# One run of small products per unit instead of two, and a reordered last group, in a linear-attention + maxout-FFN kernel

## The chip, the cores and the metric

The kernel runs on one core of a Trainium2 chip. The metric is the device time of one execution in microseconds (us); the page and the times speak of the same program, and the profiled execution has its own time. Engines are named as in the profile: PE is TensorE (matmuls), PEld its weight loads, DVE is VectorE, ACT is ScalarE, POOL is GpSimd, SP is SyncE, which here issues most of the DMAs. A label such as L870 is a line of the kernel before.

## The reference

A gated linear recurrence over 4 batches x 8 heads x 768 tokens with head size 48, followed by a feed-forward layer with a maximum of three products over the 3072 tokens that come out:

```python
f = 1 / (1 + exp(-f_logit))
for t in range(S):
    state = f[:, :, t, :, None] * state + einsum('bhd,bhe->bhde', k[:, :, t], v[:, :, t])
    y[:, :, t] = einsum('bhd,bhde->bhe', q[:, :, t], state)
x = y.transpose(0, 2, 1, 3).reshape(B * S, H * D)          # 3072 x 384
h = max(x @ w1, x @ w2, x @ w3)                            # 384 -> 768
out = h @ w_out                                            # 768 -> 384
```

## The kernel before, in words

**Units.** The recurrence is cut into chunks of 64 tokens. A unit `u` is one chunk of two batches with all eight heads; there are 24 units (`NU`), and four units make a group (`GRP`) of 512 tokens, the block that the feed-forward layer works on. Within a unit, the products of gates give scaled keys `kh` and queries `qh` (scans on DVE, multiplications on POOL from unit 6 on). With them PE does four kinds of small product, 16 matmuls each, all in fp32 with 48 or 64 rows and 64 columns, so that four of them lie in the array at a time:

- `pairs(u)` (L392): k times q inside the chunk, into the PSUM tile `a`; DVE multiplies it with the causal mask and writes `at` (L395).
- `values(u)` (L411): `at` times v, which begins the output tile `y`.
- `sums(u)` (L436): the sum over the chunk of k times v. DVE adds it to the decayed state and writes the new state (L444); `carry` (L357, POOL) makes the decayed state for the unit after the next.
- `finish(u)` (L500): the old state times `qh`, added to `y` in PSUM, and then three ACT copies (L506) of `y` into the group's input `xT`.

After a group's last unit, `pack` moves a part of `xT` by DMA (L519), and the group is ready for the feed-forward layer.

**The feed-forward work** is a generator, `ffn`. Its first half `inputs_by_pairs` (matmuls at L870) computes the three products and their maximum in a Strassen-like form with three output blocks `n`: DVE reads banks at L913 (`third`), L920 and L921 (`fourth`), ACT reads them at L878 to L905, and POOL makes sums of the result `hm` (L603). Its second half `outputs_by_pairs` (matmuls at L631, ACT reads at L636, DVE reads at L639) multiplies by `w_out`. It begins with products that need only the blocks 0 and 1 of `hm`; the "rest" products that need block 2 follow, then the sums `s1` into the banks `c` and (in the last group) `b`, then `s2` into the bank `a`, a read of `a` (`read(a, 1)`), and further products into `a`.

**Order.** Every engine works through its own queue in the order in which this program writes it. `fill(ns)` takes steps out of the pending `ffn` until a budget is used up; one fill is about 2.4 us of PE work, and a group's `ffn` is spread over 20 of them, five to a unit. In the loop over units before the change, one unit is: fill; blocks of transposed keys (L382, DVE); `finish(u-1)` and `pairs(u)`; loads; the scan for the next unit; fill; `kh` and `qh` for the next unit; fill; `values(u)` and `sums(u)`; `carry`; two more fills. So PE meets two runs of small products per unit, `finish`+`pairs` and `values`+`sums`, with two to three fills of large products between them. In the last two units there are no sums, and there `values` is followed by an ACT copy of one element, `seen` (L420), which the later `finish` has to wait for because it writes the same place of `y`. After the loop come a fill, `finish(23)`, a `pack` on two queues, and then the last group's `ffn`, between whose steps range checks of the weights (ACT, L278 and L280) are put.

[...] The loads are issued by SP in one long queue.

Of the kernel before, what the change touches and what calls it, by code (L numbers as in the profile page):

```python
# [9 lines left out]
FP32 = mybir.dt.float32  # L10
# [36 lines left out]
C = 64  # L47
# [8 lines left out]
def kernel(  # L56
# [13 lines left out]
    B, H, S, D = q.shape  # L70
    HP = H // 2
    NU = B // 2 * (S // C)
    UT = 2 * C
# [4 lines left out]
    GRP = 4  # L78
# [11 lines left out]
    def fast():  # L90
        ctx = ExitStack()
        with ctx:
# [65 lines left out]
            both = (nc.sync, nc.scalar)  # L158
# [213 lines left out]
            def keys_by_blocks(u, n):  # L372

                if BY_ROWS <= u < NU - 2:
                    kh = ready[u]["kh"]
                    if n == 0:
                        ready[u]["ks"] = work.tile([UT, H, DP], FP32, name="ks")
                    ks = ready[u]["ks"].rearrange("s (hp par) d -> s hp par d", par=2)
                    a, t0 = divmod(n * 32, C)
                    for p0 in range(0, 128, 32):  # L380
                        par, e0 = divmod(p0, DP)
                        nc.vector.transpose(ks[n * 32:(n + 1) * 32, :, par, e0:e0 + 32], kh[p0:p0 + 32, :, a, t0:t0 + 32])  # L382

            FOUR = [(par, a) for a in range(2) for par in range(2)]

            def pairs(u):
                kh, qh = ready[u]["kh"], ready[u]["qh"]
                p = ps_a.tile([UT, 2, 512], FP32, name="a")
                for hp in range(HP):
                    for par, a in FOUR:  # L390
                        r, t = slice(par * DP, par * DP + D), slice(a * C, (a + 1) * C)
                        nc.tensor.matmul(p[t, par, hp * C:(hp + 1) * C], lhsT=kh[r, hp, a, :], rhs=qh[r, a, hp, :],  # L392
                                         start=True, stop=True)
                at = work.tile([UT, 2, HP, C], FP32, name="at")
                nc.vector.tensor_tensor(at, p[:, :, 0:HP * C].rearrange("s par (h t) -> s par h t", h=HP),  # L395
                                        mask.unsqueeze(1).unsqueeze(1).to_broadcast([UT, 2, HP, C]), op=ALU.mult)
                ready[u]["at"] = at

            def values(u):
                d = ready[u]  # L400
                v_ld = v_tiles[u % NLD]
                y = ps_y.tile([128, 2, 512], FP32, name="y")
                for hp in range(HP):
                    for par, a in FOUR:
                        o, s = (par ^ a) * DP, slice(a * C, (a + 1) * C)
                        if u < GRP:
                            nc.tensor.matmul(y[s, par, hp * D:(hp + 1) * D], lhsT=d["at"][s, par, hp, :],
                                             rhs=v_ld[s, 2 * hp + par, 0:D], start=(hp == 0),
                                             stop=False, skip_group_check=True)
                            continue  # L410
                        nc.tensor.matmul(y[o:o + DP, a, hp * C:(hp + 1) * C], lhsT=v_ld[s, 2 * hp + par, :],  # L411
                                         rhs=d["at"][s, par, hp, :], start=(hp == 0),
                                         stop=False, skip_group_check=True)
                d["y"] = y
                if u >= GRP:
                    sums(u)
                if u >= NU - 2:

                    seen = work.tile([1, 1], FP32, name="seen")
                    nc.scalar.copy(seen, y[0:1, 1, (HP - 1) * C:(HP - 1) * C + 1])  # L420

            def sums(u):

                d, v_ld = ready[u], v_tiles[u % NLD]
                y = d["y"]
                if u < NU - 2:


                    apart = u < GRP
                    if apart:  # L430
                        y = ps_a.tile([128, 2, 512], FP32, name="a")
                    Y = HP * C
                    for hp in range(HP):
                        for par, a in FOUR:
                            s = slice(a * C, (a + 1) * C)
                            nc.tensor.matmul(y[par * DP:(par + 1) * DP, a, Y + hp * D:Y + (hp + 1) * D],  # L436
                                             lhsT=d["ks"][s, 2 * hp + par, :], rhs=v_ld[s, 2 * hp + par, 0:D],
                                             start=apart and hp == 0, stop=(hp == HP - 1), skip_group_check=True)
                    ds = y[:, :, Y:Y + HP * D]
                    new = states[u % 2].rearrange("p (a h) d -> p a (h d)", a=2)  # L440
                    if u < 2:
                        nc.scalar.copy(new, ds)
                    else:
                        nc.vector.tensor_tensor(new, ds, d["state"].rearrange("p (a h) d -> p a (h d)", a=2), op=ALU.add)  # L444
# [47 lines left out]
            def finish(u, xT):  # L492
                d = ready[u]
                y = d["y"]
                if u >= 2:
                    st = d["state"].rearrange("p (a h) d -> p a h d", a=2)
                    for hp in range(HP):
                        for par, a in FOUR:
                            r, o = slice(par * DP, par * DP + D), (par ^ a) * DP
                            nc.tensor.matmul(y[o:o + D, a, hp * C:(hp + 1) * C], lhsT=st[r, a, hp, :],  # L500
                                             rhs=d["qh"][r, a, hp, :], start=False, stop=(hp == HP - 1),
                                             skip_group_check=True)
                t0 = u % GRP * UT
                for par, a, n in ((0, 0, 2), (1, 1, 1), (0, 1, 1)):
                    i, o = slice(par * DP, (par + n) * DP), slice((par ^ a) * DP, ((par ^ a) + n) * DP)
                    nc.scalar.copy(xT[o, :, t0 + a * C:t0 + (a + 1) * C],  # L506
                                   y[i, a, 0:HP * C].rearrange("p (h t) -> p h t", h=HP))
                ready.pop(u)
# [105 lines left out]
            def outputs_by_pairs(g, hm, xT):  # L614
# [14 lines left out]
                def into(b, p, lhs, rhs, part=slice(None)):  # L629
                    for x, w in list(zip(lhs(p), rhs))[part]:  # L630
                        nc.tensor.matmul(b[:, p * HD:(p + 1) * HD], lhsT=x, rhs=w, start=id(b) not in begun, stop=True,  # L631
                                         skip_group_check=True)
                        begun.add(id(b))

                def read(b, n):
                    nc.scalar.copy(partial[n], b[:, 0:DM])  # L636

                def add(out, b, n, at=slice(0, 2)):
                    nc.vector.tensor_tensor(out[:, at], pairs_of(b[:, 0:DM])[:, at], pairs_of(partial[n])[:, at], op=ALU.add)  # L639

                PART_COST = HD * COLUMN
                COST, PLAIN = len(order) * PART_COST, len(lin[0]) * PART_COST
                a, b, c = bank(), bank(True), bank(True)
# [21 lines left out]
                    store_part(g, 0, 0)  # L665
                yield 2 * PART_COST
                d = b if last else c
                into(c, 0, s1, T(0))
                yield COST
                if last:  # L670
# [5 lines left out]
                else:  # L676
                    nc.scalar.copy(tops[:, 2], c[:, 0:DM])
                yield COST
                into(a, 0, s2, T(1))
                yield COST  # L680
                into(a, 1, s2, T(1))
                read(a, 1)
                yield COST
                into(a, 0, A(0, 1), T(2))
                yield COST
                into(a, 1, A(0, 1), T(2))
# [294 lines left out]
            with tc.manual_schedule():  # L981
# [78 lines left out]
                for u in range(GRP, NU):  # L1060
# [4 lines left out]
                    fill(part)  # L1065
                    keys(u)
                    keys_by_blocks(u, 2)
                    if u > GRP:
                        finish(u - 1, xT)
                        if u % GRP == 3:  # L1070
                            pack(0, 2, xT)
                        elif u % GRP == 0:
                            pack(3, 3, xT)
                    if u % GRP == 0:
# [1 line left out]
                            packed[u // GRP - 1] = xT  # L1076
                            pending.append(ffn(u // GRP - 1, xT))
                        xT = x_tiles[u // GRP % 2]
                    pairs(u)

                    if u + 2 <= BY_ROWS:
                        load(u + 2)
# [15 lines left out]
                    fill(part)  # L1098
                    if BY_ROWS < u + 2 < NU and u % GRP == 0:
                        load(u + 2, one, "k")  # L1100
                    values(u)
                    if n < NU:
                        carry(n)
                    check_range(u - CHECKS, 1)
                    fill(part)
                    if BY_ROWS < u + 2 < NU and u % GRP == 0:
                        load(u + 2, one, "q")
                    keys_by_blocks(n, 0)
                    fill(part - 1000 if u < 2 * GRP else part)
                    keys_by_blocks(n, 1)  # L1110
# [3 lines left out]
                    if BY_ROWS <= u + 2 < NU:  # L1114
                        sigmoids(u + 2)
                fill(PART)
                finish(NU - 1, xT)
                pack(3, 3, xT, both)
                packed[NU // GRP - 1] = xT
                pending.append(ffn(NU // GRP - 1, xT))  # L1120
                for n in range(NU - CHECKS, len(pieces)):
                    for step in range(3):
# [265 lines left out]
```

## Time and profile before

| what | value |
|---|---|
| median of 4 runs | 416.1 us (415.0 to 417.43) |
| the profiled execution: its own time | 415.51 us |
| its span, first to last instruction | 413.8 us |
| granted TensorE clock | 0.993 |
| PE busy | 398.5 us (96%) |
| PE weight loads busy | 332.8 us (80%) |
| DVE busy | 289.4 us (70%) |
| POOL busy | 243.6 us (59%) |
| ACT busy | 178.2 us (43%) |
| small products, busy: L392, L411, L500, L436 | 15.8, 13.9, 13.3, 11.7 us |

A line of the timeline gives the start, the time from the first start to the last end, the engine, the line, the operation, output<-inputs, shapes and the number of records; one fp32 matmul of PE leaves two records. What stands in brackets is idle time just before the line and what ended it. Matmul ends are modelled, so a cost on PE is read from start to start, and PE can be held up without a bracket.

### The profile page before, as it was taken

What the parts mean: (1) busy time and instruction counts of PE and PEld (TensorE: products, weight loads), DVE (VectorE), ACT (ScalarE), POOL (GpSimd) and SP (SyncE); (2) the same over time, 40 slices, a digit from 0 to 9 for tenths busy, and PEclk for the clock granted to TensorE, in tenths of its full rate; (3) what the DMA queues carried; (4) which work ended last, traced back from release to release, by engine and by line L of the source; (5) the groups of instructions that cost most, each with busy time, mean ns of one, the idle gap of its engine ahead of it and who ended that gap; (6) DMA issues with size and microseconds to landing.
All of it is one profiled execution on the core that took longest, in us unless ns stands there. A gap on an engine that the chain in (4) does not pass through costs nothing.

```text
span 413.8 us, 11546 instructions
## 1 busy us (share of the span) xinstructions
PE 398.5 (96%) x4598; PEld 332.8 (80%) x4598; DVE 289.4 (70%) x569; ACT 178.2 (43%) x412; POOL 243.6 (59%) x270
## 2 busy tenths in 40 slices
PE   4989999999999999999999999999999999999995
PEld 3767775566668889988889988889988898988984
DVE  6986897996775999897888977988894450002500
ACT  2487786511223431444441354523245324576210
POOL 2188694731968887487486376667466850525700
PEclk9999999999999999999999999999999999999998
DMA  8999986777456777277635376724573011641002
GB/s 170 240 274 295 260 205 87 88 150 157 79 114 85 118 129 143 41 115 90 144 78 96 55 115 86 172 56 79 73 153 88 2 55 41 153 135 59 0 21 62
DMA packets 181563, 47.21 MB, mean 114 GB/s; under 512 B 160449, under 2 KB 179201, under 8 KB 181505
## 3 DMA queue, kind: packets, MB, share of 16 engines
q1 hardware_dynamic: 178032, 45.62, 54.6%
q10 hardware_dynamic: 3472, 0.81, 0.9%
q8 instruction: 37, 0.61, 0.6%
q14 instruction: 22, 0.17, 0.2%
HBM read 37.75 MB, written 4.72 MB: 103 GB/s over the span
## 4 chain that ended last, share of the span: by engine, by line
PE 78%; SPq 7%; DVE 5%; DMA 3%; ACT 3%; issue 2%; POOL 1%; ACTq 0%; DVEq 0%; POOLq 0%
PE p L870 16%; PE p L631 14%; PE tr L870 13%; PE tr L631 11%; PE p L537 6%; PE p L563 6%; PE y L411 3%; PE y L500 2%; SPq L183 2%; PE p L776 2%; SPq L174 2%; SPq L164 2%; PE a L392 2%; PE y L436 2%; DVE ks L382 2%
## 5 line engine op out<-in xcount | busy, mean ns | idle before, releaser
L382 DVE STREAM_TRANSPOSE ks<-kh 32x128 f32<-32x128 f32 x256 | 77.4, 302 | 9.2 <-POOL kh L340 5.1
L870 PE MATMUL tr<-xT,placed 128*128 128x256 f32 x300 | 72.7, 385 | 0.2 <-DVE hm L913 0.2
L870 PEld LDWEIGHTS tr<-xT,placed 128*128 128x128 f32 x300 | 55.6, 190 | 9.3 <-ACT hm L878 1.4
L870 PE MATMUL p<-xT,placed 128*128 128x256 f32 x180 | 45.0, 381 | 0.0
L339 POOL COPY ends<-r 128x8 f32<-128x8 f32 x24 | 8.8, 366 | 49.7 <-DVE r L329 49.7
L870 PEld LDWEIGHTS p<-xT,placed 128*128 128x128 f32 x180 | 33.8, 190 | 4.7
L537 PE MATMUL p<-xT,w_in 128*128 128x256 f32 (+1 forms) x108 | 35.1, 470 | 1.5 <-POOL w_in L745 0.7
L329 DVE TENSOR_TENSOR_SCAN r<-gate,from_one 128x520 f32<-128x520 f32 x24 | 32.0, 1333 | 6.0 <-ACT gate L308 2.8
L340 POOL TENSOR_TENSOR kh<-kt,r 128x512 f32<-128x512 f32 x18 | 30.8, 1711 | 8.3 <-DVE kt L296 6.9
L639 DVE TENSOR_TENSOR o<-tr,w_in 128x384 f32<-128x384 f32 (+1 forms) x11 | 5.7, 521 | 38.6 <-PE tr L631 35.1
L603 POOL TENSOR_TENSOR w_in<-hm 128x256 f32<-128x256 f32 x15 | 11.1, 738 | 34.9 <-DVE hm L921 32.3
L347 DVE TENSOR_TENSOR_SCAN prod<-gate,from_inv 128x520 f32<-128x520 f32 x24 | 31.1, 1297 | 0.0
L506 ACT COPY xT<-y 64x256 f32<-64x256 f32 (+1 forms) x60 | 22.1, 368 | 19.3 <-PE y L500 18.1
L870 PE MATMUL p<-w_in,placed 128*128 128x256 f32 x120 | 30.0, 379 | 0.0
L913 DVE TENSOR_TENSOR hm<-tr,hm 128x512 f32<-128x512 f32 x15 | 10.3, 688 | 26.6 <-PE tr L870 19.7
L537 PEld LDWEIGHTS p<-xT,w_in 128*128 128x128 f32 x108 | 20.1, 195 | 10.4 <-issue 6.2
L636 ACT COPY w_in<-p 128x384 f32<-128x384 f32 x15 | 7.2, 477 | 45.8 <-PE p L631 45.8
L631 PE MATMUL p<-w_in,hm 128*128 128x192 f32 x120 | 25.4, 335 | 1.1 <-ACT w_in L636 1.1
L258 POOL TENSOR_TENSOR w_in<-top_bits,rest_bits 128x384 uint32<-128x384 uint32 x18 | 21.6, 1208 | 7.8 <-DVE top_bits L252 3.8
L280 ACT ACTIVATE raw<-top_bits 128x384 f32<-128x384 f32 x48 | 25.2, 526 | 0.4
L870 PEld LDWEIGHTS p<-w_in,placed 128*128 128x128 f32 x120 | 22.8, 190 | 3.1
L631 PE MATMUL tr<-w_out,w_in 128*128 128x192 f32 x120 | 24.4, 326 | 0.0
(159 smaller groups left out, 904.4 us busy)
## 6 DMA issues: line engine op xcount, KB each, us to landing
raw<-in_moe_w_dram SPq DMA_DIRECT2D x24, 384.0 KB, 4.3
v_ld<-in_v_dram SPq DMA_DIRECT2D x48, 96.0 KB, 3.2
placed<-in_moe_w_dram SPq DMA_DIRECT2D x12, 384.0 KB, 5.5
out_dram<-o SPq DMA_DIRECT2D x46, 96.0 KB, 2.2
placed<-in_moe_w_out_dram SPq DMA_DIRECT2D x6, 384.0 KB, 4.7
f_ld<-in_f_logit_dram SPq DMA_DIRECT2D x36, 64.0 KB, 2.9
k_ld<-in_k_dram SPq DMA_DIRECT2D x36, 64.0 KB, 2.8
q_ld<-in_q_dram SPq DMA_DIRECT2D x36, 64.0 KB, 2.7
```

The costliest lines, as they stand in the source:

```text
L258: nc.gpsimd.tensor_tensor(dst, by(top), by(rest), op=ALU.add)
L280: nc.scalar.activation(over, size, AF.Relu, scale=(-1 / HI_MIN, 1.0)[step - 1], bias=(1.0, -HI_END * (1 - 2.0 ** -24))[step - 1], accum_ou ...
L329: nc.vector.tensor_tensor_scan(r[:, 0:LEN][:, ::-1], flat(gate)[:, ::-1], flat(from_one)[:, ::-1], 1.0, op0=ALU.mult, op1=ALU.max)
L340: (nc.vector if u < BY_ROWS else nc.gpsimd).tensor_tensor(kh.rearrange("p h a t -> p a h t"), kt, by_batch(r[:, 1:LEN + 1].rearrange("p (x ...
L347: nc.vector.tensor_tensor_scan(flat(prod), flat(gate_tiles[u % 2]), flat(from_inv[u % 2]), 1.0, op0=ALU.mult, op1=ALU.max)
L382: nc.vector.transpose(ks[n * 32:(n + 1) * 32, :, par, e0:e0 + 32], kh[p0:p0 + 32, :, a, t0:t0 + 32])
L411: nc.tensor.matmul(y[o:o + DP, a, hp * C:(hp + 1) * C], lhsT=v_ld[s, 2 * hp + par, :], rhs=d["at"][s, par, hp, :], start=(hp == 0), stop=F ...
L506: nc.scalar.copy(xT[o, :, t0 + a * C:t0 + (a + 1) * C], y[i, a, 0:HP * C].rearrange("p (h t) -> p h t", h=HP))
L537: nc.tensor.matmul(p if w < TOK else p.rearrange("p (two t) -> p two t", two=2), lhsT=w_in[i][:, kt, j * 128:(j + 1) * 128], rhs=x[:, t.st ...
L563: nc.tensor.matmul(p[:, 0:DM], lhsT=lhsT, rhs=rhs, start=(n == 0), stop=(n == NJ + NK - 1))
L631: nc.tensor.matmul(b[:, p * HD:(p + 1) * HD], lhsT=x, rhs=w, start=id(b) not in begun, stop=True, skip_group_check=True)
L870: nc.tensor.matmul(b[:, j * HALF:(j + 1) * HALF], lhsT=w[:, (2 * n + j) * 128:(2 * n + j + 1) * 128], rhs=x, start=begin and j == 0, stop= ...
```

## The change

It does three things.

1. `values(u-1)` and `sums(u-1)` leave the middle of unit `u-1` and go to the top of unit `u`, into one run: `values(u-1)`, `sums(u-1)`, `pairs(u)`, `finish(u-1)`. For this, the sums go into the free columns of the PSUM tile of `pairs` (`room_of_unit`) instead of those of `y`, and the DVE addition that writes the state is split off (`new_state`) and called inside `finish`, behind the mask multiplication. Since `values` and `finish` now stand in one run, `seen` is issued for every unit from 4 on.
2. In the last unit `values(23)` stays where it was, and `finish(23)` with its `pack` moves two fills ahead, so that two fills and the check steps lie between it and the last `ffn`.
3. In the last group's `outputs_by_pairs`, the two steps of `s2` with `read(a, 1)` (new function `second`) go ahead of the two steps of `s1`. In the other groups the order stays.

```diff
-            def pairs(u):
+            def pairs(u, p=None):
...
-                if u >= GRP:
-                    sums(u)
-                if u >= NU - 2:
+                if u >= GRP:
                     seen = work.tile([1, 1], FP32, name="seen")
                     nc.scalar.copy(seen, y[0:1, 1, (HP - 1) * C:(HP - 1) * C + 1])
...
-            def sums(u):
+            def sums(u, p=None):
...
+                    d["sums"] = y = room_of_pairs() if p is None else p
...
-                                             start=apart and hp == 0, stop=(hp == HP - 1), skip_group_check=True)
+                                             start=True, stop=True)
+                    if p is None:
+                        new_state(u)
...
             def finish(u, xT):
...
+                new_state(u)
...
+                def second():
+                    for p in range(2):
+                        into(a, p, s2, T(1))
+                        if p:
+                            read(a, 1)
+                        yield COST
...
+                if last:
+                    yield from second()
                 into(c, 0, s1, T(0))
...
-                into(a, 0, s2, T(1))
-                yield COST
-                into(a, 1, s2, T(1))
-                read(a, 1)
-                yield COST
+                if not last:
+                    yield from second()
...
                     keys_by_blocks(u, 2)
+                    room_of_unit = room_of_pairs()
+                    if u > GRP:
+                        values(u - 1)
+                        sums(u - 1, room_of_unit)
+                    pairs(u, room_of_unit)
                     if u > GRP:
                         finish(u - 1, xT)
...
-                    pairs(u)
...
-                    values(u)
                     if n < NU:
                         carry(n)
+                    else:
+                        values(u)
...
+                    if n == NU:
+                        finish(u, xT)
+                        pack(3, 3, xT, both)
+                        packed[u // GRP] = xT
...
                 fill(PART)
-                finish(NU - 1, xT)
-                pack(3, 3, xT, both)
-                packed[NU // GRP - 1] = xT
                 pending.append(ffn(NU // GRP - 1, xT))
```

More of the change, by code (lines that the diff above doesn't have):

```diff
@@ L384, in fast, with room_of_pairs @@
             FOUR = [(par, a) for a in range(2) for par in range(2)]
-            def pairs(u):
+            def room_of_pairs():
+                return ps_a.tile([128, 2, 512], FP32, name="a")
+            def pairs(u, p=None):
                 kh, qh = ready[u]["kh"], ready[u]["qh"]
-                p = ps_a.tile([UT, 2, 512], FP32, name="a")
+                if p is None:
+                    p = room_of_pairs()
                 for hp in range(HP):
@@ L415, in values @@
                 if u >= GRP:
-                    sums(u)
-                if u >= NU - 2:
                     seen = work.tile([1, 1], FP32, name="seen")
                     nc.scalar.copy(seen, y[0:1, 1, (HP - 1) * C:(HP - 1) * C + 1])
-            def sums(u):
+            def sums(u, p=None):
                 d, v_ld = ready[u], v_tiles[u % NLD]
-                y = d["y"]
                 if u < NU - 2:
-                    apart = u < GRP
-                    if apart:
-                        y = ps_a.tile([128, 2, 512], FP32, name="a")
+                    d["sums"] = y = room_of_pairs() if p is None else p
                     Y = HP * C
@@ L437, in sums, with new_state @@
                                              lhsT=d["ks"][s, 2 * hp + par, :], rhs=v_ld[s, 2 * hp + par, 0:D],
-                                             start=apart and hp == 0, stop=(hp == HP - 1), skip_group_check=True)
-                    ds = y[:, :, Y:Y + HP * D]
+                                             start=True, stop=True)
+                    if p is None:
+                        new_state(u)
+            def new_state(u):
+                d = ready[u]
+                if u < NU - 2:
+                    ds = d["sums"][:, :, HP * C:HP * (C + D)]
                     new = states[u % 2].rearrange("p (a h) d -> p a (h d)", a=2)
```

## The prediction

> **What bounds the kernel now.** I read the page first: PE is busy 96% of the span, and its waits add up to 9.6 us, 8.3 of them before 50 us. So time is gained only where PE has less to do, or where PE is held up without a bracket.
>
> Second, the timeline of PE over unit 18 and at the two units where `values` stands alone:
>
> ```profile
> 256.06 1.03 PE L870 MATMUL p<-w_in,placed 128*128 128x256 f32 x4
> 257.02 0.66 PE L500 MATMUL y<-qh,state 48*48 48x64 f32 x32
> 257.50 0.65 PE L392 MATMUL a<-qh,kh 48*64 48x64 f32 x32
> 258.08 1.99 PE L870 MATMUL tr<-xT,placed 128*128 128x256 f32 x8
> ...
> 262.50 1.03 PE L870 MATMUL tr<-xT,placed 128*128 128x256 f32 x4
> 263.46 0.69 PE L411 MATMUL y<-at,v_ld 64*64 64x64 f32 x32
> 263.97 0.63 PE L436 MATMUL y<-v_ld,ks 64*64 64x48 f32 x32
> 264.54 1.99 PE L870 MATMUL tr<-xT,placed 128*128 128x256 f32 x8
> 266.37 1.03 PE L870 MATMUL p<-xT,placed 128*128 128x256 f32 x4
> ...
> 336.82 0.49 PE L631 MATMUL tr<-w_in,xT 128*128 128x192 f32 x2
> 337.24 0.69 PE L411 MATMUL y<-at,v_ld 64*64 64x64 f32 x32
> 337.87 0.92 PE L631 MATMUL p<-w_out,hm 128*128 128x192 f32 x4
> 338.62 0.49 PE L631 MATMUL p<-w_in,xT 128*128 128x192 f32 x2
> ```
>
> A large record costs 0.216 us (256 columns) or 0.1625 (192) from start to start. What a run takes beyond the large work beside it: `values`+`sums` from 262.50+4x0.216=263.36 to 266.37-8x0.216=264.64: 1.28 us. `finish`+`pairs`, reckoned likewise: 1.26. `values` alone, 337.145 to 338.62-0.65=337.97: 0.83; the lone `finish(23)` at 346.51: 0.83. So an added `sums` costs 0.45, an added `pairs` 0.43, and a run by itself about 0.33 beyond its products (0.83 against the 0.48 to 0.52 that `finish` or `values` takes to the next product inside a run).
>
> Third, the timelines around 161 us and the end:
>
> ```profile
> 134.68 0.71 DVE L296 STREAM_TRANSPOSE qt<-q_ld 128x512 f32<-128x512 f32 x1 [2.52 <-DMA out_dram<-o]
> ...
> 161.26 0.68 DVE L921 SCALAR_TENSOR_TENSOR hm<-hm,top_bits 128x512 f32<-128x512 f32 x1
> ```
> ```profile
> 160.91 0.49 PE L631 MATMUL tr<-w_in,xT 128*128 128x192 f32 x2
> 161.40 1.20 PE L631 MATMUL p<-w_out,hm 128*128 128x192 f32 x4
> 162.43 0.81 PE L631 MATMUL tr<-w_out,hm 128*128 128x192 f32 x4
> ```
> ```profile
> 398.07 0.48 ACT L636 COPY w_in<-p 128x384 f32<-128x384 f32 x1 [2.28 <-PE p L631]
> 398.60 0.92 PE L631 MATMUL p<-w_in,hm 128*128 128x192 f32 x4 [0.57 <-ACT w_in L636]
> ```
>
> DVE waits 2.52 us for a q load and from 134.68 to 161.94 has no idle line; SP issues loads without a gap from 50 to 140 us, one each 0.6 us, so that load's time does not depend on PE. At 161.40 PE's four "rest" records take 1.03 us instead of 0.65: they wait for `hm` from L920/L921. Here, in unit 11, load queue and DVE hold PE, and what PE saves before it is lost. The last fence: `s2` ends, ACT reads `a`, PE stands 0.57 us.
>
> **The change part by part.**
>
> *The merged run.* One run of four products: 1.28+1.26-0.33=2.21 us. The 0.33 is known at both ends only: 0 if the switching goes on between the products of one run, 0.40 if an inner `values` costs what an inner `pairs` does (0.83-0.43). I take 0.33, read from the same two products.
>
> Before the point at 162 us, DVE's stretch keeps its contents: the state additions L444 of units 9 and 10 (0.52 us each) move inside it, at 135.31 and 148.25, and stay inside it. So the rest products still wait until 161.94, and everything saved in units 5 to 11 goes. So does the new stall of unit 5: there `seen` queues behind five ACT instructions ending with the key copy L369 (68.30 to 68.88); `finish(4)` could start 1.40 us after `values`, at about 68.0, and would start at 69.0. It costs 1.0 us, and the stretch covers it; uncovered, it is added.
>
> From 162 us on, the small work before is: `finish`+`pairs` of unit 12 with its stall, 168.28 to 169.70: 1.42; `values`+`sums` of unit 12, likewise 1.35; nine units of 1.26+1.28=22.86; unit 22, 1.26+0.83; unit 23, 1.26. Together 28.98. After: units 12 to 22, 11x2.21=24.31, and unit 23 without sums, 1.76: 26.07. The lone `values(23)` and `finish(23)` cost the same on both sides. Gain 2.91 us; the part is small because `values(11)` and `sums(11)` now fall behind the point. With 0 saved per merge the same sum is a loss of 1.05, with 0.40 a gain of 3.75.
>
> *The added wait.* `finish(u-1)` waits for `seen`, and `seen` stands in ACT's queue ahead of the copies L506 and all later reads of banks. At 323.06 `values` starts and `seen` runs 323.82 to 323.97, 0.91 after; `finish` follows `values` by 0.52+0.45+0.43=1.40. Slack 0.49, so I cost it at nothing. Before units 16 and 20 ACT also has a 0.48 us read (228.32 to 228.80, from 0.11 into the run); it ends before `values` does. Its cover gone, it costs the excess in each run.
>
> *The moved state addition* now stands ahead of the next unit's scans: 0.52 us later for `qh`. `qh` was ready 1.2 us before `pairs` in units 16 and 20 (227.49 against 228.70) and 2.8 to 6.7 elsewhere after unit 12; `pairs` itself comes 0.48 later in its run, units are 0.33 shorter: 0.8 us left. DVE's `hm` for the rest products of unit 15 had 1.4 us to spare (220.53 against 221.95); the state addition and a PE path shorter by 0.33 leave 0.6. Nothing is charged. At unit 12 `pairs` stands 0.97 into the run and meets `qh` (168.93) without the old stall. SP: `pack` waits for copies that end some 0.9 us later in the run, and loads and stores queue behind it; unit 18's k load was waited for 0.17 us by a DVE chain with 5 us left. POOL's `carry` gets its state half a unit ahead.
>
> *The last unit.* `finish(23)` stood, at 346.51, between `s2` and the product that needs `a` read, and hid that read. Moved, it uncovers the stall that the last group shows: +0.67 (0.57, and 0.10 because the next records start slower after an empty array: 398.60 to 399.35 is 0.75, not 0.65). Against it, the stall of 0.55 at 351.87, where ACT was late behind the L506 copies and a DMA issue of 0.72, shrinks to about 0.1: -0.56.
>
> *The last group.* With `s1` (2.6 us) behind `s2`, the read of `a` is covered: -0.67. But `s2` now follows `read(a, 0)` (392.22 to 392.70), and PE could start it at 392.67: +0.18. The DVE sums of `xT` and POOL's `s2` (389.8) are ready. Both last parts together: +0.11-0.49=-0.38.
>
> Sum: -2.91-0.38=-3.3, on the profiled 415.51 us (span 413.8 and 1.7 around it): 412.2. That execution stands 0.6 below the median, so 412.8.
>
> [...]
>
> L921 of one shape took 684 to 1707 ns in this trace, so the point may move by 1.0 either way.
>
> **The rivals.**
>
> 1. *The point gives way.* For: DVE's stretch contains one 1.71 us L921. Against: the q load's time is SP's. If nothing binds there, 19 merges of 0.33 count, less unit 5's 1.0, plus the last parts: -6.3+1.0-0.4=-5.7, 410.4 us by the median.
> 2. *The switching stays, inside the run* (64-row products next to 48-row ones). For: no row shows these two kinds side by side. +1.05-0.38=+0.7: 416.8 us, no measurable change.
> 3. *Slower: `finish` waits for ACT in each merged run.* Twelve runs after the point each pay what ACT is late beyond 0.49 us; from 0.28 us late the gain is gone. For: ACT does steps of 0.5 to 0.6 us, in order, and unit 5 shows the case. Against: at units 13 to 23 ACT is idle or in its last step at the run's start. At 0.5: +6.0-3.3=+2.7, 418.8 us.
>
> **How the numbers follow.** Forecast 0.55, rival 1 0.12, rival 2 0.18, rival 3 0.15. The forecast's own range is 411.5 to 414.2 (0.25 to 0.40 saved, the point moving by 0.7). Over 0.5% (2.1 us, about what a measurement can tell) is faster below 414.0: most of the forecast (0.50) and rival 1: 0.61; within: the rest of it and rival 2: 0.23; slower: rival 3: 0.16. The range from 410.6 to 417.0 leaves out rival 3 and part of rival 1.
>
> **What would show it.** Right: one run per unit, about 2.2 us by the same reckoning, large products uninterrupted for five fills; L920/L921 of unit 11 and the rest products still near 162 us; no bracket on L500 but in unit 5 and, where ACT waits for L921, unit 11; no wait after the last `s2`, one in group 4. Wrong: brackets or gaps ahead of L500 in every unit, a run of 2.5 us, or rest products well before 161 us.

## The result and the profile after

The changed kernel takes 415.87 us (median of 52 runs, 413.02 to 417.66), the kernel before 416.57 us (78 runs, 414.4 to 419.17). The ratio is 0.9979, interval 0.997 to 0.9988: 0.9 us faster by the ratio, 0.7 by the two medians, and less than the 0.5% from which the prediction would have called it faster. 412.8 us was forecast. The profiled execution took 415.81 us, with a span of 414.1 us against 413.8 before: 0.3 us longer, where the sum of the prediction was 3.3 us shorter.

The merged run itself came out as predicted. The timeline of PE over unit 17 of the kernel after (the columns are those of the lines before: start, time, engine, line, operation, shapes and records, idle time):

```profile
241.93 1.03 PE L881 MATMUL tr<-xT,placed 128*128 128x256 f32 x4
242.89 0.69 PE L415 MATMUL y<-at,v_ld 64*64 64x64 f32 x32
243.40 0.63 PE L433 MATMUL a<-v_ld,ks 64*64 64x48 f32 x32
243.85 0.66 PE L396 MATMUL a<-qh,kh 48*64 48x64 f32 x32
244.34 0.63 PE L504 MATMUL y<-qh,state 48*48 48x64 f32 x32
244.89 1.13 PE L881 MATMUL tr<-xT,placed 128*128 128x256 f32 x4
245.86 1.03 PE L881 MATMUL p<-xT,placed 128*128 128x256 f32 x4
247.26 2.86 PE L881 MATMUL tr<-xT,placed 128*128 128x256 f32 x12 [0.37 <-ACT hm L889]
```

From 241.93+4x0.216=242.79 to 245.86-4x0.216=245.00 is 2.20 us for four products in one run (2.21 predicted), where the two runs before cost 1.26 and 1.28. But the last line shows something that was not there before: eight records behind the run, PE stands 0.37 us for L889, an ACT read of a bank.

The view of PE's waits after, by line and by the line waited for (us in total, times, longest):

```profile
PE y L504 <- ACT seen L422: 2.3, 2, 1.6
...
PE tr L881 <- ACT hm L889: 1.1, 3, 0.4
PE a L396 <- POOL qh L351: 1.0, 1, 1.0
...
PE p L542 <- ACT hm L807: 0.7, 2, 0.3
PE p L636 <- ACT w_in L641: 0.6, 1, 0.6
```

`finish` waits for `seen` twice, in units 5 and 11, not in every unit. In unit 10 `pairs` waits for `qh`, which POOL makes from the q load that DVE waits for. The wait in the last group is gone, one in group 4 is left.

Where the time came from and went is read from the start of the first large record behind the run that has `pairs(u)`, kernel after minus kernel before. The last column compares the two kernels with the obstacles out of the way; it belongs to the experiments.

| at unit | after - before, us | e8_all - e5_late_before, us |
|---|---|---|
| 9 | +0.02 | -0.03 |
| 10 | +0.81 | -0.24 |
| 11 | +2.21 | -0.57 |
| 12 | +2.49 | -0.80 |
| 13 | +2.28 | -0.94 |
| 14 | +2.41 | -1.25 |
| 16 | +1.76 | -1.91 |
| 17 | +1.61 | -2.05 |
| 18 | +1.74 | -2.37 |
| 20 | +1.07 | -3.03 |
| 21 | +0.93 | -3.17 |
| 22 | +1.06 | -3.48 |
| 23 | +0.75 | -3.80 |
| last matmul | +0.32 | -5.09 |

By unit 11 the kernel after is 2.21 us behind; at the point at 162 us 1.71 of that is left, as shown below. At unit 12 it is 2.49, because the run there also holds `values(11)` and `sums(11)`, which the kernel before had done at 158.10, ahead of the point. From unit 12 on it gains 0.33 us per unit, but not in every unit: from 12 to 13, 16 to 17 and 20 to 21 it gains only 0.14 to 0.21, and from 13 to 14, 17 to 18 and 21 to 22 it loses 0.13.

The lines of the kernel after that answer to those around 161 us, first DVE, then PE:

```profile
135.47 0.71 DVE L296 STREAM_TRANSPOSE qt<-q_ld 128x512 f32<-128x512 f32 x1 [3.00 <-DMA out_dram<-o]
...
139.94 1.30 DVE L932 SCALAR_TENSOR_TENSOR hm<-hm,top_bits 128x512 f32<-128x512 f32 x1
...
152.38 1.74 DVE L932 SCALAR_TENSOR_TENSOR hm<-hm,top_bits 128x512 f32<-128x512 f32 x1 [0.35 <-POOL top_bits L917]
...
162.58 0.69 DVE L932 SCALAR_TENSOR_TENSOR hm<-hm,top_bits 128x512 f32<-128x512 f32 x1
```
```profile
154.89 0.97 PE L504 MATMUL y<-qh,state 48*48 48x64 f32 x32 [1.56 <-ACT seen L422]
155.79 2.07 PE L881 MATMUL p<-rest_bits,placed 128*128 128x256 f32 x4
157.65 1.45 PE L881 MATMUL p<-w_in,placed 128*128 128x256 f32 x4
...
163.49 0.81 PE L636 MATMUL p<-w_out,hm 128*128 128x192 f32 x4
164.14 0.81 PE L636 MATMUL tr<-w_out,hm 128*128 128x192 f32 x4
```

The record that stood at 162.43 before now stands at 164.14: 1.71 us later. Three things make it up. The q load is in at 135.47 instead of 134.68, 0.79 later. DVE's stretch from there to the end of the last L932 takes 163.27-135.47=27.80 us instead of 161.94-134.68=27.26, 0.54 more. And PE did not have to wait at 163.49: it came 0.38 us later than DVE would have let it go (the record after L932 followed 0.49 after its end before, 162.43-161.94; 163.27+0.49=163.76 against 164.14). Why PE was late there is told in the last section: its granted clock was 0.50 from 155.4 to 158.4.

### The profile page after: what moved, and what is told of

Read it like the earlier page. It is cut to its first block, busy times and chain, and to the rows that moved or that the text cites. A ratio compares the mean times of both kernels' runs of the same rounds, so it can differ in the third digit from the quotient of the medians.

```text
span 414.1 us, 11516 instructions
## 1 busy us (share of the span) xinstructions
PE 393.1 (95%) x4598; PEld 332.4 (80%) x4598; DVE 295.0 (71%) x569; ACT 180.6 (44%) x430; POOL 246.8 (60%) x270
## 4 chain that ended last, share of the span: by engine, by line
PE 85%; DVE 5%; ACT 3%; POOL 3%; issue 2%; DMA 0%; SPq 0%; DVEq 0%; POOLq 0%; ACTq 0%
PE p L881 17%; PE p L636 15%; PE tr L881 14%; PE tr L636 11%; PE p L542 7%; PE p L568 6%; PE p L787 3%; PE y L415 3%; PE a L396 2%; PE y L504 2%; PE a L433 2%; DVE ks L382 1%; POOL w_in L258 1%; DVE r L329 1%; PE y L411 1%
## 5 line engine op out<-in xcount | busy, mean ns | idle before, releaser
L881 PE MATMUL tr<-xT,placed 128*128 128x256 f32 x300 | 71.6, 384 | 1.1 <-ACT hm L889 1.1
L542 PE MATMUL p<-xT,w_in 128*128 128x256 f32 (+1 forms) x108 | 34.0, 459 | 3.4 <-POOL w_in L756 1.9
L329 DVE TENSOR_TENSOR_SCAN r<-gate,from_one 128x520 f32<-128x520 f32 x24 | 33.0, 1375 | 6.0 <-ACT gate L308 2.8
L542 PEld LDWEIGHTS p<-xT,w_in 128*128 128x128 f32 x108 | 19.5, 190 | 12.7 <-issue 6.0
L641 ACT COPY w_in<-p 128x384 f32<-128x384 f32 x15 | 7.2, 479 | 42.2 <-PE p L636 42.2
```

Source lines behind the costliest of these rows:

```text
L329: nc.vector.tensor_tensor_scan(r[:, 0:LEN][:, ::-1], flat(gate)[:, ::-1], flat(from_one)[:, ::-1], 1.0, op0=ALU.mult, op1=ALU.max)
L542: nc.tensor.matmul(p if w < TOK else p.rearrange("p (two t) -> p two t", two=2), lhsT=w_in[i][:, kt, j * 128:(j + 1) * 128], rhs=x[:, t.st ...
L881: nc.tensor.matmul(b[:, j * HALF:(j + 1) * HALF], lhsT=w[:, (2 * n + j) * 128:(2 * n + j + 1) * 128], rhs=x, start=begin and j == 0, stop= ...
```

## Experiments

All were timed in five rounds beside the kernel before.

**The two parts alone.** e1_merge_only is the kernel after with the old order in the last group:

```diff
-                if last:
-                    yield from second()
                 into(c, 0, s1, T(0))
...
-                if not last:
-                    yield from second()
+                yield from second()
```

e2_tail_only is the kernel before with the new order in the last group:

```diff
+                if last:
+                    into(a, 0, s2, T(1))
+                    yield COST
+                    into(a, 1, s2, T(1))
+                    read(a, 1)
+                    yield COST
                 into(c, 0, s1, T(0))
...
-                into(a, 0, s2, T(1))
...
-                yield COST
...
+                if not last:
+                    into(a, 0, s2, T(1))
+                    yield COST
...
```

> The change without its third part: in the last group s1 stays ahead of s2. Theory (each of the two parts is worth what the rows said): the stall of 0.57 us ahead of the product that follows the last s2 is back and the time is 0.5 us above the changed kernel, some 0.4 us below the kernel before (ratio 0.999). Rival (the reorder is hidden by the end of the kernel, or the merge alone carries the gain): equal to the changed kernel, ratio 0.998.

> The kernel before with the third part alone: s2 ahead of s1 in the last group. Theory: the 0.57 us wait after the last s2 goes, a wait of up to 0.2 us ahead of s2 comes, 0.5 us below the kernel before (ratio 0.9988). Rival: the wait reappears further on in the same group (another read of the same bank, the last store), no difference (1.000).

e1_merge_only: 415.91 us, ratio 0.9986 (0.9969 to 1.0002). e2_tail_only: 416.14 us, ratio 0.9991 (0.9972 to 1.001). Neither time tells from no change; the traces do. The timeline of PE in e1_merge_only has the old wait:

```profile
397.93 0.49 PE L636 MATMUL p<-w_in,w_in 128*128 128x192 f32 x2
398.99 0.92 PE L636 MATMUL p<-w_in,hm 128*128 128x192 f32 x4 [0.57 <-ACT w_in L641]
```

and the kernel after, whose lines have `s1` there, has not:

```profile
398.69 0.49 PE L636 MATMUL tr<-w_out,w_in 128*128 128x192 f32 x2
399.02 0.81 PE L636 MATMUL p<-w_in,hm 128*128 128x192 f32 x4
```

From `finish(23)` to the last matmul it is 67.81 us in e1_merge_only (340.89 to 408.70) and 67.22 in the kernel after (341.41 to 408.63): the last group is worth 0.59, in e2_tail_only against before 61.23 to 61.80: 0.57. Predicted: 0.49.

These two gave something else. In e2_tail_only, which has the order of before at 162 us, the q load came in at 136.61, 1.93 us later than in the profiled execution of before, and its span is 415.1 us:

```profile
136.61 0.71 DVE L296 STREAM_TRANSPOSE qt<-q_ld 128x512 f32<-128x512 f32 x1 [1.78 <-DMA out_dram<-o]
```
```profile
164.36 0.81 PE L631 MATMUL tr<-w_out,hm 128*128 128x192 f32 x4
```

So the load's time is not one number. What the kernels differ in is the way from the load to the record behind the point:

| profiled execution | q load in | record behind the point | between |
|---|---|---|---|
| before | 134.68 | 162.43 | 27.75 |
| e2_tail_only (runs apart) | 136.61 | 164.36 | 27.75 |
| e1_merge_only (merged) | 135.33 | 163.63 | 28.30 |
| e6_check (merged) | 135.59 | 163.86 | 28.27 |
| after (merged) | 135.47 | 164.14 | 28.67 |

The 0.54 of DVE belongs to the merge: it is there in all three merged executions, and not in the two with the runs apart. Nothing ties the 0.79 of the load to the merge: the latest load of the five is in an execution with the runs apart; what sets it stays open. The 0.38 is in one execution alone: in e1_merge_only and e6_check `finish` waited for `seen` just as long (1.55 and 1.53 us), and yet PE was early enough to wait for DVE, as the timeline of PE in e1_merge_only shows:

```profile
154.76 0.67 PE L504 MATMUL y<-qh,state 48*48 48x64 f32 x32 [1.55 <-ACT seen L422]
...
162.60 1.19 PE L636 MATMUL p<-w_out,hm 128*128 128x192 f32 x4 [0.70 <-DVE hm L928]
163.63 0.81 PE L636 MATMUL tr<-w_out,hm 128*128 128x192 f32 x4
```

So the wait for `seen` in unit 11 is covered by DVE's, and costs nothing by itself here.

**The load out of the way.** In both kernels (e4_late_after from the kernel after, e5_late_before from the kernel before) the eight stores of group 0's outputs are put behind later DMAs in SP's queue, so that the k and q loads are issued earlier:

```diff
                             nc.scalar.copy(o, p[:, 0:DM])
-                            store(i, o)
+                            late.append((i, o))
```

> The changed kernel with the first group's eight output stores put off until its q load for units 10 and 11 is issued; nothing else moves, and the q load is issued some 4.6 us earlier. Theory (the SP queue holds DVE until 135 us, DVE holds an ACT read of a bank in unit 11, and seen and finish(10) stand behind that read): the waits of 1.0 us (unit 10) and 1.6 us (unit 11) go and with them 3 to 4.6 us, ratio to the kernel before about 0.989. Rival (the stall at unit 11 is made by the moved state addition and by the run itself, whatever the loads do): the 1.6 us wait stays and less than 1 us is gained, ratio 0.996.

> The kernel before with the same eight stores put off. Theory: it had held-up products of 0.2, 0.2, 0.15, 0.4 and 0.15 us between 137 and 169 us, so it gains about 1.1 us (ratio 0.997), much less than the changed kernel does by the same edit; the difference between the two kernels grows from 0.9 to 3.5 us or more. Rival: the load was no bound in either kernel, both gain the same, 0 to 0.5 us.

e4_late_after: 411.59 us (411.02 to 412.24), ratio 0.9875 (0.9853 to 0.9896), span 410.0. e5_late_before: 414.44 us (413.93 to 414.72), ratio 0.9944 (0.9925 to 0.9962), span 412.7. SP's issue of the q load in the kernel after (the last column counts the DMAs):

```profile
128.69 4.51 SPq L183 DMA_DIRECT2D q_ld<-in_q_dram  x8
```

and in e4_late_after, with DVE's transposition of q and PE's run in unit 11:

```profile
123.78 5.21 SPq L183 DMA_DIRECT2D q_ld<-in_q_dram  x8
```
```profile
131.74 0.71 DVE L296 STREAM_TRANSPOSE qt<-q_ld 128x512 f32<-128x512 f32 x1 [1.63 <-DMA q_ld<-in_q_dram]
```
```profile
150.59 0.69 PE L415 MATMUL y<-at,v_ld 64*64 64x64 f32 x32
...
152.04 0.63 PE L504 MATMUL y<-qh,state 48*48 48x64 f32 x32
152.60 1.13 PE L881 MATMUL p<-rest_bits,placed 128*128 128x256 f32 x4
```

The load is 3.7 us earlier, the waits of units 10 and 11 are gone, and with the load earlier in both kernels the change as a whole, last group included, is worth 414.44-411.59=2.85 us, three times what it brought with it, but less than the 3.5 expected. The kernel before gains 2.2 us by the medians and 1.1 by the spans of the profiled executions (412.7 against 413.8), as expected; the rest may be that the profiled execution of before had an early load.

The load may also be what spreads the times: 12 runs of e2_tail_only lie 4.1 us apart and 52 of the kernel after 4.6 us, but 5 and 6 of these two 1.2 and 0.8 us, and 12 of e13_split below, which has late stores too, 1.2. It is not shown: 12 runs of e1_merge_only, with the load where it was, lie only 2.4 apart, and 5 of e8_all below, with late stores, 1.8.

**The range checks behind a fill.** The waits for L889 follow only the runs of units 13, 17 and 21. The kernel after, ACT in unit 17:

```profile
243.65 0.15 ACT L422 COPY seen<-y 1x1 f32<-1x1 f32 x1 [0.93 <-PE y L415]
245.03 1.13 ACT L511 COPY xT<-y 128x256 f32<-128x256 f32 x3 [1.23 <-PE y L504]
246.18 0.55 ACT L278 ACTIVATE top_bits<-raw 128x384 f32<-128x384 f32 x1
246.64 0.57 ACT L889 COPY hm<-tr 128x512 f32<-128x512 f32 x1
```

and the kernel before:

```profile
242.95 1.13 ACT L506 COPY xT<-y 128x256 f32<-128x256 f32 x3 [0.90 <-PE y L500]
244.10 0.56 ACT L278 ACTIVATE top_bits<-raw 128x384 f32<-128x384 f32 x1
244.57 0.56 ACT L878 COPY hm<-tr 128x512 f32<-128x512 f32 x1
```

Before, `finish` opened the run and `pairs` ran beside the copies, so the read of the bank ended at 245.13, and PE went on at 245.19. Now `finish` closes a run that is nearly twice as long: the copies start 2.14 us after the run did (245.03 against 242.89; before, 242.95 against 242.22, 0.73), the check step stands between them and the read, and PE goes on when the read has ended, at 247.21. e6_check is the kernel after with the check step moved behind the fill:

```diff
+                    fill(part)
                     check_range(u - CHECKS, 0)
-                    fill(part)
```

> The changed kernel with the first step of the range check (an ACT instruction of 0.55 us, L278) written behind the next fill instead of ahead of it. Theory (in units 13, 17 and 21 finish's three ACT copies now end 0.5 us later against PE, the check step stands behind them, and the read of a bank that PE needs for the fifth product stands behind both): the three waits of 0.38 us on that read go, with 0.08 to 0.1 each for the slower restart, 1.4 us in all, ratio to the kernel before 0.9945. Rival (the copies alone make ACT late, the check step is not needed for it): the waits only shrink, under 0.5 us is gained, ratio 0.997.

414.14 us (413.1 to 414.67), ratio 0.9934 (0.9913 to 0.9955), span 412.5. The timeline of PE in unit 17:

```profile
245.13 1.03 PE L881 MATMUL p<-xT,placed 128*128 128x256 f32 x4
246.10 2.86 PE L881 MATMUL tr<-xT,placed 128*128 128x256 f32 x12
```

All three waits are gone. Of the 1.6 us of span, 0.28 was gained at the point (163.86 against 164.14, where the kernel after had been late by its clock) and the rest behind it, 0.43 to 0.44 per wait: 0.37 or 0.38 and a slower restart. So the rival of the expectation, that the copies alone make ACT late, is out.

**The price of a run, by itself.** e13_split is e4_late_after with the merged run cut again, between `sums` and `pairs`, half of the fill on each side:

```diff
-                    fill(part)
+                    fill(part / 2 if u > GRP else part)
                     keys(u)
...
                         sums(u - 1, room_of_unit)
+                        fill(part / 2)
                     pairs(u, room_of_unit)
```

> The changed kernel with the late stores, and the merged run cut in two: half of the unit's first fill stands between the sums and the pairs, so that PE does the same work in the same queue order but for large products between the two halves of each of 19 runs. Theory (a run costs 0.33 us beyond its products, paid where PE changes between small and large products): 19 x 0.33 = 6.3 us more than with the late stores alone (411.6), some 417.5 us, ratio 1.002. Rival (the gain of the late stores comes from other waits, and a run by itself costs next to nothing): within 1 us of 411.6 us, ratio 0.988 to 0.99.

416.96 us (416.84 to 418.04), ratio 1.0012 (0.9997 to 1.0028), span 415.2: 5.2 us more than e4_late_after by the spans, 5.4 by the medians. The timeline of PE in unit 16:

```profile
225.65 0.49 PE L636 MATMUL p<-w_in,w_in 128*128 128x192 f32 x2
226.07 0.70 PE L415 MATMUL y<-at,v_ld 64*64 64x64 f32 x32
226.59 0.63 PE L433 MATMUL a<-v_ld,ks 64*64 64x48 f32 x32
227.15 0.92 PE L636 MATMUL p<-w_in,w_in 128*128 128x192 f32 x4
227.90 0.49 PE L636 MATMUL p<-w_in,xT 128*128 128x192 f32 x2
```

The first half takes 227.90-4x0.1625-(225.65+2x0.1625)=1.28 us, as `values` and `sums` did before; `pairs` and `finish` follow at 228.65 and take 1.27. Read point by point as in the table above, e13_split falls behind e4_late_after by 0.34 us in each of the units 6, 8 to 11 and 13 to 23. The others have their own reasons: unit 7 had no fill left to put between; in unit 5 the cut also takes away the wait for `seen` (0.74 in e4_late_after); and at unit 12 it meets no hold of the rest products, where in e4_late_after the four of them take from 159.01 to 160.04, 0.38 more than four such records do. That makes 5.2 where 19x0.33=6.3 was expected. With the same products in the same order, 0.34 us is the price of entering and leaving a run, apart from every wait.

So a run with large products on both sides costs 0.33 us (before) to 0.34 us (e13_split) beyond its products. What PE does in this time, no run shows.

**All together.** e8_all is the kernel after with the late stores, the check behind the fill, and `s2` ahead of `s1` in the last two groups. Beside the edits shown for e4_late_after and e6_check:

```diff
-                if last:
+                if g >= NU // GRP - 2:
                     yield from second()
...
-                if not last:
+                if g < NU // GRP - 2:
                     yield from second()
```

> The changed kernel with the late stores of the first group, the check step behind the next fill, and s2 ahead of s1 in the last but one group too. Theory: the gains add up, since each removes its own wait: 5.0 us for the stores as measured, 1.4 us for the check step, 0.6 us for the uncovered read of the last but one group: 7.0 us under the kernel before, ratio 0.983. Rival (with those waits gone DVE or POOL holds PE at the next place): 0.986 or above, with new waits on DVE in the trace.

409.86 us (409.22 to 410.98), ratio 0.9843 (0.982 to 0.9866), span 407.6: the best of all, 6.5 us under the kernel before beside it (416.35) where 7.0 was expected. From 76 us on PE has no bracket at all. The right column of the table above sets it against e5_late_before, which has the early load too: from unit 13 on, 0.31 to 0.33 us are gained in every unit but 13, 17 and 21, where it is 0.14. What is missing there, 0.19 three times, is a read of the bank `a` (`read(a, 2)`), which the middle run of units 12, 16 and 20 used to cover. In the kernel after, the timeline of PE in unit 16 shows it without a bracket, and that of PEld, the weight loads, with one:

```profile
234.38 0.81 PE L636 MATMUL tr<-w_in,xT 128*128 128x192 f32 x4
235.11 0.92 PE L636 MATMUL p<-w_in,hm 128*128 128x192 f32 x4
235.87 0.49 PE L636 MATMUL p<-mix,xT 128*128 128x192 f32 x2
```
```profile
235.11 0.62 PEld L636 LDWEIGHTS p<-w_in,hm 128*128 128x128 f32 x4 [0.21 <-ACT w_in L641]
```

234.38+4x0.1625=235.03, so PE stands 0.08 us, and the four records then take 0.76 instead of 0.65: 0.19 together. ACT reads `a` at L641 from 234.58 to 235.06, and the trace names this read as what the weight load waited for; the same bracket of 0.21 stands in units 12 (176.18) and 20 (294.04). A run that removes this wait alone was not made.

Taking `seen` away was not tried: it is there to order the products of `values` and `finish` that add to the same place of `y`, and no run shows what becomes of them without it.

## Why the prediction was right and wrong

**Right: the merged run.** 2.20 us against 2.21, and 0.33 saved in every unit where nothing else comes in (e8_all), and 0.34 lost again when it is cut (e13_split). By its time alone, 415.87 us, the result looks like rival 2 (416.8), in which the switching stays inside the run; the run of 2.20 us, where that rival needs 2.54, rules it out.

**Right: the added wait after the point.** The slack of 0.49 us for `seen` held in units 12 to 22; rival 3 did not come. In unit 5 the wait cost 0.71 where 1.0 was reckoned. In unit 11 ACT waited for L932 (its L916 began at 154.21 and `seen` at 154.69), as the prediction's last paragraph allowed, and DVE covered it.

**Right: the end.** The last group gave 0.57 to 0.59 (0.49 predicted); the last unit lost what is left between that and the 0.43 from unit 23 to the last matmul, 0.14 to 0.16 (0.11 predicted).

**Wrong: "Nothing is charged", the later copies.** The prediction said that the copies L506 now end some 0.9 us later in the run and followed this to `pack`, SP and the loads. It did not follow what stands behind them in ACT's own queue: a check step in one unit of four, then the bank read L878 (now L889) that frees the fifth product. Three times 0.46 (1.40 us for four records in unit 17 of the kernel after, 0.94 before): 1.4 us. This is the largest term that was missed; e6_check gave it back, but for some 0.03 each.

**Wrong: a run that was taken away was charged only what it cost.** For the last unit the prediction saw that a run of small products also hides a bank read from PE. The same holds for the middle runs of units 12, 16 and 20, and there it was not looked for: 3x0.19=0.6 us. Units 4 and 5 show it once more: `PE p L542 <- ACT hm L807`, two waits of 0.35 at 59.76 and 74.90, stands in the kernel after alone; before, `values` and `sums` ran shortly ahead of these products (59.45 and 73.05). In the kernel after this costs nothing in the end, since the point comes behind it.

**Wrong in size: "DVE's stretch keeps its contents".** It keeps them, but takes 0.54 us more: the L932 at 139.94 took 1.30 us instead of 0.83 (+0.47), the one at 152.38 waited 0.35 for POOL's L917, and against that a scan (L329) at 160.59 took 1.24 instead of 1.60 (-0.36); the rest is small. The same three stand in e1_merge_only and e6_check. The prediction let the point move by 1.0 us either way, but put nothing for it in the sum.

**Luck of one execution.** The load's time is SP's, as said, but SP's time is spread over 1.9 us between executions of the same instructions (134.68 and 136.61), and the sum was made on the profiled execution with the earliest load, whose 415.51 us lie 1.06 below the median of 78 runs. The prediction added 0.6 for that, from the four runs it had.

The sum again, against the profiled execution: -3.3 +1.4 +0.6 +0.5 (DVE) +0.8 (load) +0.4 (PE's clock) = +0.4; the spans differ by +0.3. If the load and the clock are alike on both sides by the median, which five traces cannot show, -3.3 +1.4 +0.6 +0.5 = -0.8 is left; measured are 0.9 by the ratio and 0.7 by the medians. Of the 3.1 us between the forecast of 412.8 and 415.87, these three terms are 2.5, and 0.5 is that 78 runs put the kernel before at 416.57, not 416.1.

Rival 1, where the point gives way, is nearly what the late stores made of the two kernels. It reckoned 5.7 us for the change; e5_late_before to e4_late_after is 2.85. The price of 0.33 per merge held, but the rival had left out the same two reads (2.0 us); the two waits for L807 left next to nothing saved by unit 9, where it had 0.65; and at the point DVE still held the rest products of e4_late_after for 0.38.

## What to carry to other kernels

When a step is moved within its engine's order, its consumer moves too, on another engine, and pushes back what stands behind it there (here the copies began 2.14 us into the run instead of 0.73, and PE lost 1.4 us to the reads behind them): walk down that engine's queue to the first instruction that PE will wait for, and look at it in every unit, since here only one in four had the extra step in front. A run that is taken away also takes away the cover that it gave (here 0.19 us in each of three units); look for the read that it hid. And before summing on one execution, see how far its late loads stand from those of another: here the gain could be measured as 0.9 us or as 2.9, with the same PE work, by whether a group's stores stood before a load or behind it.

## What was not expected of the hardware

In the kernel after, PE's clock fell to half in unit 11, in one execution. The columns of the view by windows are the stretch and its length, the busy time of PE, PEld, DVE, ACT and POOL (records in brackets), the granted clock, and the share and GB/s of the DMA engines; the kernel after, then e1_merge_only:

```profile
155.00:157.50 2.50, 2.50 (x36) 2.09 (x37) 2.40 (x8) 1.53 (x4) 2.42 (x4) 0.52 0.68 187
157.50:159.00 1.50, 1.50 (x6) 1.18 (x6) 1.47 (x4) 0.74 (x3) 1.42 (x4) 0.67 0.18 49
```
```profile
155.00:157.50 2.50, 2.50 (x42) 2.21 (x31) 2.42 (x7) 1.91 (x5) 2.42 (x4) 1.00 0.76 204
157.50:159.00 1.50, 1.50 (x12) 1.50 (x11) 1.47 (x4) 0.36 (x2) 1.42 (x4) 1.00 0.19 49
```

In steps of 0.6 us the clock is 0.74 from 154.8, 0.50 from 155.4 to 158.4, and 0.92 then: half speed for 3.0 us and less than full speed in the step on either side, right after a stand of 1.56 us between small products. In it L504 took 0.97 us (0.67 in e1_merge_only) and the four large records behind it 1.86 instead of 0.96. It cost PE 1.6 us, of which DVE's wait hid all but 0.38. The same stand in e1_merge_only (1.55 us) and in e6_check (1.53 us) left the clock at 1.00. What brought it down in this one execution, no run shows.

POOL and DVE: L932, one shape, took 0.69 us at 162.58, 1.30 at 139.94 and 1.74 at 152.38. In the last case POOL's L899 ran from 152.30 to 153.57, and L932 ended 0.55 us behind it; at 139.94 L899 ran from 139.42 to 140.69, and L932 ended 0.55 us behind it too. At 162.58 POOL was idle. In the kernel before, POOL's L888 ended at 139.89 and 152.30, and the L921 begun at 139.61 and 151.15 ended at 140.44 and 152.86, 0.55 and 0.56 us behind it; at 161.26, with POOL idle, L921 took 0.68. Why DVE's instruction ends that far behind POOL's, no run shows.
